# Sparse attention with global tokens and a feed-forward: global scores of a quad in one operation with band scores

## The chip, the cores and the metric

The kernel runs on one core of a Trainium2 chip. The metric is the device time of one execution in microseconds, from three runs: the median is compared. The trace is one further execution, recorded by the hardware profiler.

## The reference

Eight batches of eight heads; each head has 512 local and 32 global tokens of 64 values. A local query sees the local keys at most 32 positions away and all 32 global keys; a global query sees every key. What comes out, 4352 rows of 512 values, goes through a feed-forward layer with 2048 hidden values.

```python
def _attn_ref(q_l, k_l, v_l, q_g, k_g, v_g):
    ...
    k_all = np.concatenate([k_g, k_l], axis=2)
    v_all = np.concatenate([v_g, v_l], axis=2)
    s_g = scale * np.matmul(q_g, k_all.transpose(0, 1, 3, 2))
    out_g = np.matmul(sm(s_g), v_all)
    s_ll = scale * np.matmul(q_l, k_l.transpose(0, 1, 3, 2))
    mask = np.abs(pos[:, None] - pos[None, :]) <= window
    s_ll = np.where(mask, s_ll, -1000000000.0)
    s_lg = scale * np.matmul(q_l, k_g.transpose(0, 1, 3, 2))
    a_l = sm(np.concatenate([s_lg, s_ll], axis=-1))
    out_l = np.matmul(a_l, v_all)
    return np.concatenate([out_g, out_l], axis=2)

def _moe_ref(x, w_in, w_out):
    h = x @ w_in
    g = h - np.tanh(h)
    return g @ w_out
```

`sm` is the softmax over the last axis.

## The kernel before

**Tiling.** Two heads make a pair, so there are 32 pairs, `pairs[0]` to `pairs[31]`, four to a batch; two pairs make a quad. The feed-forward works in chunks: one for each batch's 512 local rows and one, at the end, for the 256 global rows of all batches. A chunk of 512 rows has 16 steps; a step has twelve hidden matmuls (line 1219, or 1245 in the earliest steps) and twelve output matmuls (line 1282), each of 512 columns: the float32 operands are split in a high and a low part, and three of the four products are made. Between the two stand ACT's tanh (1227), DVE's subtraction (1230), a rounding copy (363, ACT mostly) and the rest, taken on POOL (1236). The attention of batch b+1 runs among the feed-forward of batch b.

**Attention from the ninth pair on** (`j >= OWN`, `OWN` is 8). For each pair, `add_keys` and `add_queries` transpose the raw keys and queries on DVE (697, 709). `add_band_scores` (713) makes the local scores: a block of 32 queries against 96 local keys and the 32 global keys, 32 matmuls of 64 rows, 32 stationary columns and 128 moving columns, in two operations, the first of two 128-row tiles and the second of the other two; the scores of the two heads stand in two banks. `add_band` (1126) follows with peak (DVE, 1132), exponential (ACT, 1137), inverse (DVE) and scaling (POOL, 1146), and transposes the result (DVE, 1152), which DMAs move to where the products read it. For each quad, `Quad.add_halves` (955) makes the scores of the global queries of its four heads, 16 matmuls in the same 64-row, 32-column shape, eight with 256 moving columns and eight with 32 (line 972), in two further banks, and then peak (DVE, 982 and 985), exponential (ACT, 993), inverse and scaling (POOL, 1003). `add_global_turn` (779) transposes them on DVE (793, 795), and `add_products` (800) multiplies all probabilities of a pair by its values (830). The trace counts two records for each of these matmuls: 64 for a pair's band, 32 for a quad's global scores.

**Earlier pairs.** Pairs 4 to 7 use the same band scores, but other global scores (`add_scores`, 1016, with the matmuls at 1030) and other products (814). Pairs 0 to 3 have a path of their own (`first_attention`: 547, 656, 1176).

**Banks.** There are eight banks of matmul results. Operations ask for banks from a named set (line 356): attention of later batches from `att`, banks 0 to 2; hidden layer from `h`, banks 0 to 3; output layer from `acc`, banks 4 to 7.

**The order.** No operation is issued where the program names it. Each is handed to `add` with its engine and estimated time, what it reads and writes, the banks that it takes and frees, and a due time. `Order.run` (115) then simulates the engines and repeatedly takes the operation with the earliest start (plus a small share of its due time), and the instructions are issued in that order on each engine's queue. A bank is handed out only when whoever held it has been placed with all that read it. Going from one tile shape of TensorE to another is charged by `switch` (101): `MW` for the way back to the full array, `MV` for others. When TensorE would idle early on, `filler` (1507) puts matmuls without use in the gap. The due times and weights are the constants of `CFG` (343): names that begin with `o_` and end in 0, 1 or 2 are the offsets of attention in the first batch, the second and all later ones (`o_l`: band scores, `o_g`: global scores), and the rest set weights loading, the steps of the feed-forward, and which engine is preferred for a copy.

`attention(j)` (1389) names the operations of a pair in sequence; where two of them touch the same buffer, this sequence decides which is first. For odd `j` it names, after the keys, the quad's global scores, the turning and products of the pair before, and then the queries and the band scores of pair `j`.

Of the kernel before, what the change touches and what calls it, by code (L numbers as in the profile page):

```python
# [217 lines left out]
def kernel(ctx, tc, q_l, k_l, v_l, q_g, k_g, v_g, w_in, w_out, out):  # L218
# [3 lines left out]
    NT = S // P  # L222
    T = S + G
# [12 lines left out]
    OWN = 8  # L236
# [94 lines left out]
    def bank(shape, j, dt=F32):  # L331
# [6 lines left out]
        elif len(shape) == 4:  # L338
# [1 line left out]
        return t  # L340


    CFG = dict(a_g=-20, a_kg=8.6471, a_ph=-0.3776, a_qs=3.1395, a_w=0.1186, a_wn=0.3468, a_xg=106.4499, d_g=3.1804, d_kg=30.2528, d_ph=13.5028,
               d_qh=26.732, d_qs=-2.8448, d_tg=-7.2746, d_tp=19.0976, d_w=27.3757, d_wn=73.5687, d_xg=31.5443, d_y=19.0351, gfirst=0, ho=4086.9099,
               hs=1945.7008, lag=2058.0703, last=-656.3726, newb=2, p0=1174.4585, pen=-2.1431, penp=-16.7696, s_g=37.3966, s_w=10.8784,
               step=4056.6186, step1=117.929, lag0=-6898.385, hs0=174.1645, tol=0.0001449392, wd0=3738.22, wsp=-399.3218, xw=0.07263301,
               o_ld0=6998.8548, o_tn0=-70.3794, o_tg0=4900.3517, o_s0=-8488.5413, o_sp0=-1339.9745, o_t0=-7480.9842, o_vl0=-4568.2292,
               o_pv0=-6980.563, wsp1=-266.4844, ho0=4731.2006, mw=0.2696114, o_h0=9000, hp=-9000, bp0=8995.7209, bp1=-7509.0482, bp2=-3805.4551,
               bp3=-9000, p_w=150, p_kg=-0.4636, mv=0.0001195388, kd=3.441514e-05, a_sq=8.5297, o_gb=8757.2134, o_kl2=-2217.8445, o_ql2=7034.0784,
               o_kt2=-7538.1981, o_qt2=-1378.049, o_l2=-5351.7965, o_lp2=-2940.782, o_g2=-2834.6403, o_tg2=-1206.1443, o_sq2=-696.1794,  # L350
               o_vl2=5851.8969, o_pv2=8097.3484, o_kl1=2328.5123, o_ql1=5480.9611, o_kt1=-1133.8937, o_qt1=-1536.1301, o_l1=-8243.7002,
               o_lp1=4742.1478, o_g1=7959.6348, o_tg1=7293.7765, o_sq1=6170.1166, o_vl1=-3483.3411, o_pv1=310.4111, o_g0=-5056.3219, p_bd=33.4845)

    PHASE = [{k[:-1]: v for k, v in CFG.items() if k.startswith("o_") and k.endswith(x)} for x in "012"]

# [1 line left out]
    add = order.add  # L357
# [142 lines left out]
    class Pair:  # L500
# [209 lines left out]

            add(("D", 0.69), turn, self.due(self.C["o_qt"]), r=["kq"], w=["hk0"])

        def add_band_scores(self, *ranges):
            kw, u = keys[self.u], self.u
            s = [(f"s{a.two}", a.i) for a in self.heads]
            box = {}

            def mm(tiles):
                def fn(e, tags):
                    if "s" not in box:  # L720
                        box["s"] = [bank([P, NT, SQ], tags[x]) for x in s]
                        for a in self.heads:
                            a.scores = box["s"][a.two]
                    for t in tiles:
                        for c in range(4):
                            n = NT * t + c - 1
                            at = G * (2 + 3 * (n // 2) + n % 2 if n >= 0 else 0)
                            for a in self.heads:
                                r = slice(a.e, a.e + D)
                                nc.tensor.matmul(box["s"][a.two][G * c:G * c + G, t], query()[r, t * P + G * c:t * P + G * c + G],  # L730
                                                 kw()[r, at:at + SQ], start=True, stop=True)
                return fn

            for j, tiles in enumerate(ranges):
                add(("T", 0.222 * len(tiles)), mm(tiles), self.due(self.C["o_l"] + self.C["o_lp"] * j), r=[f"kw{u}", f"kg{u}", "hk0"], w=s,
                    res=["p00", "p10"],
                    alloc=[(x, "att") for x in s] if j == 0 else (), rows=0.8, ldw=0.027, tail=0.107, mode=3)
            for a in self.heads:
                a.add_band(self)
# [208 lines left out]
    class Quad:  # L948
# [3 lines left out]
            self.m, self.pairs = m, pairs[2 * m:2 * m + 2]  # L952
            self.sn = 2 * (m % 2)

        def add_halves(self):
            a, b, c, d = [stats[self.sn + i][:, j:j + 2] for i in range(2) for j in (12, 14)]
            sg, sh, st = ("sg", self.m, "q"), ("sh", self.m, "q"), ("st", self.sn)
            all_ = ["pg0", "pg1", "pl0", "pl1"]
            box = {}
            C = self.pairs[0].C  # L960

            def mm(e, tags):
                box["s"] = y = [bank([P, 9 * G], tags[n]) for n in (sg, sh)]
                for lo, n in ((0, 8 * G), (8 * G, G)):
                    for x in self.pairs:
                        for half in range(2):
                            p0 = 64 * x.u + G * half
                            for r in range(2):
                                rows = slice(64 * r, 64 * r + 64)
                                k = keys[x.u]()[rows]  # L970
                                k = k[:, G:2 * G] if lo else view(k[:, :1], [(3 * G, 4), (1, 2 * G)], 2 * G + 12 * G * half)
                                nc.tensor.matmul(y[r][p0:p0 + G, lo:lo + n], gqs()[rows, 0, x.jj, r], k, start=True, stop=True)  # L972

            def swap(dst, src):
                for q in range(4):
                    p = slice(32 * q, 32 * q + 32), slice(32 * (q ^ 1), 32 * (q ^ 1) + 32)
                    nc.vector.tensor_copy(dst[p[0]], src[p[1]])  # L977

            def peak(e, _):
                zero = masks[1][:, WIN:WIN + 1]  # L980
                for r in range(2):
                    nc.vector.tensor_tensor_reduce(out=pgh[:, r, G:9 * G], in0=box["s"][r][:, :8 * G], in1=zero.broadcast_to([P, 8 * G]), scale=-0.125,
                                                   scalar=1e30, op0=ALU.add, op1=ALU.min, accum_out=a[:, r:r + 1])
                for r in range(2):
                    nc.vector.tensor_tensor_reduce(out=pgh[:, r, 9 * G:], in0=box["s"][r][:, 8 * G:], in1=only_first, scale=-0.125,
                                                   scalar=a[:, r:r + 1], op0=ALU.add, op1=ALU.min, accum_out=b[:, r:r + 1])
                swap(c, b)
                nc.vector.tensor_tensor(a, b, c, op=ALU.min)

            def exp(e, _):  # L990
                for r in range(2):
                    x = pgh[:, r, G:]
                    nc.scalar.activation(x, x, AF.Exp, bias=a[:, r:r + 1], scale=-1.0, accum_out=c[:, r:r + 1])

            def inverse(e, _):
                swap(b, c)
                nc.vector.scalar_tensor_tensor(d, c, 1e-9, b, op0=ALU.add, op1=ALU.add)
                nc.vector.reciprocal(b, d)

            def norm(e, _):  # L1000
                for r in range(2):
                    x = pgh[:, r, G:]
                    nc.gpsimd.tensor_scalar(x, x, b[:, r:r + 1], 1.0, op0=ALU.mult, op1=ALU.mult)

            def due(off):
                return self.pairs[1].due(C["o_g"] + off)

            reads = [f"{n}{u}" for n in ("kw", "kg") for u in range(2)] + ["gq"]
            pool = self.pairs[0].tag
            add(("T", 0.53), mm, due(0), r=reads, w=[sg], res=all_, alloc=[(sg, pool), (sh, pool)], ldw=0.027, tail=0.027, rows=0.8, mode=3)  # L1010
            add(("D", 2.05), peak, due(1), r=[sg, ("mask", 1), "of"], w=all_ + [st], free=[(sg, 1), (sh, 1)])
            add(("A", 1.15), exp, due(1.5), r=[st], w=all_)
            add(("D", 1.1), inverse, due(2), r=["pg0"], w=[st])
            add(("P", 1.25), norm, due(2.5), r=[st], w=all_)

        def add_scores(self):
            if self.m >= OWN // 2:
                return self.add_halves()
            s = stats[self.sn]
            sg, sh, st = ("sg", self.m, "q"), ("sh", self.m, "q"), ("st", self.sn)  # L1020
            all_ = ["pg0", "pg1", "pl0", "pl1"]
# [367 lines left out]
    def attention(j):  # L1389
        order.land = LAND  # L1390
        x = pairs[j]
        if j == OWN:
            add_gaps()
        x.add_keys()
        if j % 2:
            quad = Quad(j // 2)
            quad.add_scores()
            pairs[j - 1].add_global_turn()
            pairs[j - 1].add_products(0, 1)
        x.add_queries()  # L1400
        x.add_band_scores(*(range(2), range(2, NT)))
        if j + 1 < NH // 2:
            if (j + 1) % (H // 2) == 0:
                add_globals((j + 1) // (H // 2))
            pairs[j + 1].add_raw()
        if j % 2 == 0:
            x.add_values()
        x.add_squares()
        if j % 2:
            x.add_values()  # L1410
            x.add_global_turn()
            x.add_products(0, 1)
# [133 lines left out]
```

## Time and profile before

| what | value |
|---|---|
| median of three runs | 904.38 us (903.88 to 907.87) |
| profiled execution, its own time | 905.91 us |
| its span, first to last instruction | 904.1 us |
| TensorE (PE) busy | 892.7 us, 99% |
| VectorE (DVE) busy | 481.7 us, 53% |
| ScalarE (ACT) busy | 372.5 us, 41% |
| GpSimd (POOL) busy | 338.9 us, 37% |
| granted TensorE clock, mean | 0.993 |

Busy is the union of an engine's instructions. Matmuls overlap, so a busy TensorE is not one at its peak: how far it comes is read from the distance between the starts of successive groups. Times of a timeline count from the span's first instruction.

### The profile page before, as it was taken

The numbers are of one execution on the slowest core, as the hardware profiler recorded it, in microseconds if no ns is written. First come the engines' busy times: TensorE is split into PE (matmuls) and PEld (weight loads), VectorE is DVE, ScalarE is ACT, GpSimd is POOL, SyncE is SP. The second block draws the span as 40 slices with busy tenths as digits, with TensorE's granted clock in tenths as the row PEclk, the third lists the DMA queues.
The fourth block names the chain that finished last, engine by engine and source line by source line (L and its number), as shares of the span: only waits on it lengthen the run. The fifth ranks groups of instructions, "written<-read, shape, count | busy, mean of one in ns | idle before, by whom it ended". The sixth has DMA issues, their size and how long they took to land.

```text
span 904.1 us, 23449 instructions
## 1 busy us (share of the span) xinstructions
PE 892.7 (99%) x9100; PEld 719.8 (80%) x9100; DVE 481.7 (53%) x1820; ACT 372.5 (41%) x1035; POOL 338.9 (37%) x504
## 2 busy tenths in 40 slices
PE   8999999999999999999999999999999999999998
PEld 6678787787878888787878888788878888888896
DVE  6889977835638383745638373746637362111110
ACT  6877764434344333533343333533344242322221
POOL 5567665333333233333333233423223231222121
PEclk9899999999999999999999999999999999999999
DMA  9877774934555434555555434545454302100000
GB/s 207 192 185 204 205 182 98 226 92 112 107 135 139 101 85 112 142 117 116 103 153 116 109 84 111 144 114 119 95 147 112 95 35 61 47 1 1 36 13 23
DMA packets 286959, 101.14 MB, mean 112 GB/s; under 512 B 254848, under 2 KB 277376, under 8 KB 286848
## 3 DMA queue, kind: packets, MB, share of 16 engines
q1 hardware_dynamic: 284800, 98.53, 45.5%
q8 instruction: 71, 1.16, 0.5%
q10 hardware_dynamic: 2048, 1.11, 0.4%
q14 instruction: 40, 0.33, 0.1%
HBM read 76.01 MB, written 21.50 MB: 108 GB/s over the span
## 4 chain that ended last, share of the span: by engine, by line
PE 92%; DVE 4%; ACT 2%; issue 1%; DMA 1%; POOL 0%; ACTq 0%; DVEq 0%; POOLq 0%
PE bank L1282 40%; PE bank L1219 39%; PE bank L830 4%; PE bank L730 3%; PE bank L814 2%; PE bank L1245 1%; PE bank L656 1%; PE bank L1176 1%; PE bank L972 1%; DVE turned L793 1%; DVE stats L977 1%; DMA raw<-in_q_l_dram 1%; DVE t L1230 0%; ACT prob L1137 0%; PE bank L547 0%
## 5 line engine op out<-in xcount | busy, mean ns | idle before, releaser
L1236 POOL TENSOR_TENSOR gates<-t,gates 128x512 fp32r<-128x512 f32 x136 | 175.1, 1288 | 394.0 <-PE bank L1282 245.7
L1282 PE MATMUL bank<-w_out_hi,gates 128*128 128x512 f32 x1088 | 297.2, 393 | 0.9 <-ACT gates L363 0.9
L1282 PEld LDWEIGHTS bank<-w_out_hi,gates 128*128 128x128 f32 x1088 | 202.3, 188 | 46.9 <-issue 2.9
L1230 DVE TENSOR_TENSOR t<-bank,t 128x512 f32<-128x512 f32 x136 | 92.8, 684 | 238.8 <-ACT t L1227 238.3
L1227 ACT ACTIVATE t<-bank 128x512 f32<-128x512 f32 x136 | 80.7, 594 | 232.2 <-PE bank L1219 231.2
L363 ACT CAST gates<-t 128x512 fp32r<-128x512 f32 x136 | 84.3, 622 | 166.9 <-PE bank L1282 92.8
L1282 PE MATMUL bank<-w_out_lo,gates 128*128 128x512 f32 x544 | 150.8, 391 | 0.0
L1219 PE MATMUL bank<-x_hi,w_in_hi 128*128 128x512 f32 x432 | 123.4, 401 | 0.0
L1282 PEld LDWEIGHTS bank<-w_out_lo,gates 128*128 128x128 f32 x544 | 102.0, 188 | 21.8 <-issue 0.2
L1219 PE MATMUL bank<-x_lo,w_in_hi 128*128 128x512 f32 x432 | 118.6, 390 | 0.0
L1219 PE MATMUL bank<-x_hi,w_in_lo 128*128 128x512 f32 x432 | 118.5, 390 | 0.0
L1146 POOL TENSOR_SCALAR prob<-prob,stats 128x128 f32<-128x128 f32 x224 | 79.0, 372 | 82.5 <-DVE stats L1142 43.7
L1137 ACT ACTIVATE prob<-prob,stats 128x128 f32<-128x128 f32 x224 | 86.9, 390 | 22.8 <-DVE stats L1132 22.8
L1219 PEld LDWEIGHTS bank<-x_lo,w_in_hi 128*128 128x128 f32 x432 | 81.0, 188 | 17.7 <-issue 0.2
L1219 PEld LDWEIGHTS bank<-x_hi,w_in_lo 128*128 128x128 f32 x432 | 80.9, 188 | 17.8 <-issue 0.2
L1219 PEld LDWEIGHTS bank<-x_hi,w_in_hi 128*128 128x128 f32 x432 | 77.8, 188 | 19.3 <-issue 2.8
L793 DVE STREAM_TRANSPOSE turned<-pg 32x96 f32<-32x96 f32 x288 | 77.7, 270 | 8.5 <-PE bank L830 1.7
L1132 DVE CUSTOM_DVE_ANT_0 prob<-bank,band 128x128 f32<-128x128 f32 x224 | 49.7, 286 | 28.1 <-PE bank L730 28.1
L1152 DVE STREAM_TRANSPOSE sq<-prob 128x512 f32<-128x512 f32 x50 | 35.3, 708 | 51.3 <-POOL prob L1146 48.7
L1137 ACT ACTIVATION_READ_ACCUMULATOR prob<-prob,stats 128x1 f32 x224 | 42.1, 188 | 0.0
L830 PEld LDWEIGHTS bank<-turned 128*32 128x32 f32 x3072 | 33.4, 111 | 8.9 <-issue 5.7
L830 PE MATMUL bank<-turned 128*32 128x32 f32 (+1 forms) x3072 | 37.2, 206 | 0.1
(157 smaller groups left out, 900.1 us busy)
## 6 DMA issues: line engine op xcount, KB each, us to landing
moved<-sq SPq DMA_DIRECT2D x24, 512.0 KB, 2.8
turned<-in_v_l_dram SPq DMA_DIRECT2D x23, 512.0 KB, 5.4
turned<-in_v_l_dram SPq DMA_DIRECT2D x32, 256.0 KB, 3.5
out_dram<-wraw SPq DMA_DIRECT2D x32, 256.0 KB, 2.1
rawkq<-in_k_l_dram SPq DMA_DIRECT2D x112, 64.0 KB, 2.6
rawkq<-in_q_l_dram SPq DMA_DIRECT2D x112, 64.0 KB, 2.4
turned<-in_v_g_dram SPq DMA_DIRECT2D x48, 128.0 KB, 4.6
turned<-moved SPq DMA_DIRECT2D x48, 128.0 KB, 2.9
```

Of the source, the lines that this page charges most:

```text
L363: (nc.scalar.copy if e == "A" else eng[e].tensor_copy)(dst, src)
L793: nc.vector.transpose(win_g[G * g:G * g + G, a.two, 3 * x:3 * x + 3], view(pgh[r, a.two, G * (j + x):G * (j + x) + 1], [(3 * G, 3), (1, G)]))
L830: m = nc.tensor.matmul(y, win_v[:, NW * a.two + w, G * d:G * d + G], x, start=n == 0, stop=n == 7, skip_group_check=True)
L1132: nc.vector.tensor_tensor_reduce(out=x[:, t], in0=self.scores[:, t], in1=bands[0 if t == 0 else 2 if t == NT - 1 else 1], scale=-0.125, sc ...
L1137: nc.scalar.activation(x[:, t], x[:, t], AF.Exp, bias=self.st[:, t:t + 1], scale=-1.0, accum_out=self.st[:, 4 + t:5 + t])
L1146: nc.gpsimd.tensor_scalar(x[:, t], x[:, t], self.st[:, 8 + t:9 + t], 1.0, op0=ALU.mult, op1=ALU.mult)
L1152: nc.vector.transpose(z[:, :, self.two].rearrange("p n t c -> p t n c"), x[:, :, k * n * G:(k + 1) * n * G].rearrange("p t (n c) -> p t n ...
L1219: nc.tensor.matmul(self.h[s][:, j * n:(j + 1) * n], w[:, cc, f * P:(f + 1) * P], self.x()[xi](cc)[:, :n], start=part == 0 and cc == 0 and ...
L1227: nc.scalar.activation(tt_[q], self.h[s], AF.Tanh)
L1230: nc.vector.tensor_sub(tt_[q], self.h.pop(s), tt_[q])
L1236: eng[e].tensor_sub(gg[q][1], tt_[q].rearrange("p (k c) -> p k c", k=4), f32(gg[q][0]))
L1282: nc.tensor.matmul(self.acc[tt], g[:, j * nt + tt], low_out(f) if wi else w_out_hi[:, f], start=s == 0 and k == 1, stop=last and k == 3 * ...
```

## The change

Global scores of the quads from the ninth pair on (twelve quads, at odd `j` from 9 to 31) are no longer an operation of their own. `add_band_scores` of the quad's second pair hands its matmuls, all four tiles at once, to `add_halves`, which issues them and then the global scores in one operation. This operation asks for four banks of the set `h`, where there were two of `att` for each. Its due time is that of the band scores. In `attention`, the quad's turning and products of its first pair are named after the band scores of the second. Band scores of the first pair of a quad stay as two operations, and so do all of the pairs before the ninth. All constants of `CFG` that set the order get other values, also those of the first batch and of the loading of weights; of those lines one is shown.

```diff
-               o_pv0=-6980.563, wsp1=-266.4844, ho0=4731.2006, mw=0.2696114, o_h0=9000, hp=-9000, bp0=8995.7209, bp1=-7509.0482, bp2=-3805.4551,
+               o_pv0=-698.2739, wsp1=-397.8031, ho0=6683.6544, mw=0.6734363, o_h0=1583.6807, hp=-2528.881, bp0=8787.3597, bp1=-7359.1769,
...
-        def add_band_scores(self, *ranges):
+        def add_band_scores(self, *ranges, quad=None):
...
-            for j, tiles in enumerate(ranges):
+            if quad:
+                quad.add_halves(mm(range(NT)), self.due(self.C["o_l"]), s, [f"kw{u}", f"kg{u}", "hk0"])
+            for j, tiles in enumerate(() if quad else ranges):
                 add(("T", 0.222 * len(tiles)), mm(tiles), self.due(self.C["o_l"] + self.C["o_lp"] * j), r=[f"kw{u}", f"kg{u}", "hk0"], w=s,
...
-        def add_halves(self):
+        def add_halves(self, scores, at, s, more):
...
-            pool = self.pairs[0].tag
-            add(("T", 0.53), mm, due(0), r=reads, w=[sg], res=all_, alloc=[(sg, pool), (sh, pool)], ldw=0.027, tail=0.027, rows=0.8, mode=3)
+            def both(e, tags):
+                scores(e, tags)
+                mm(e, tags)
+
+            add(("T", 0.888 + 0.53), both, at, r=reads + more, w=[sg] + s, res=all_ + ["p00", "p10"], alloc=[(x, "h") for x in s + [sg, sh]],
+                ldw=0.027, tail=0.027, rows=0.8, mode=3)
...
         def add_scores(self):
-            if self.m >= OWN // 2:
-                return self.add_halves()
...
         if j % 2:
             quad = Quad(j // 2)
-            quad.add_scores()
+            if j < OWN:
+                quad.add_scores()
+                pairs[j - 1].add_global_turn()
+                pairs[j - 1].add_products(0, 1)
+        x.add_queries()
+        x.add_band_scores(*(range(2), range(2, NT)), quad=quad if j % 2 and j >= OWN else None)
+        if j % 2 and j >= OWN:
             pairs[j - 1].add_global_turn()
             pairs[j - 1].add_products(0, 1)
-        x.add_queries()
-        x.add_band_scores(*(range(2), range(2, NT)))
```

## Rows read from the trace of the kernel before

**Rows 1.** The page, chain that ended last, by engine and by line.

```profile
PE 92%; DVE 4%; ACT 2%; issue 1%; DMA 1%; POOL 0%; ACTq 0%; DVEq 0%; POOLq 0%
PE bank L1282 40%; PE bank L1219 39%; PE bank L830 4%; PE bank L730 3%; PE bank L814 2%; PE bank L1245 1%; PE bank L656 1%; PE bank L1176 1%; PE bank L972 1%; DVE turned L793 1%; DVE stats L977 1%; DMA raw<-in_q_l_dram 1%; DVE t L1230 0%; A
```

**Rows 2.** Windows: stretch, length, busy us by engine, granted clock, DMA share, GB/s.

```profile
0.00:60.60 60.60, 54.43 (x444) 40.84 (x444) 46.71 (x195) 45.33 (x129) 33.76 (x70) 0.92 0.87 198
...
140.00:760.30 620.30, 619.30 (x7269) 496.87 (x7267) 345.83 (x1374) 236.08 (x703) 214.78 (x339) 1.00 0.49 115
...
37.00:46.00 9.00, 8.70 (x51) 6.38 (x53) 7.58 (x36) 7.21 (x22) 5.75 (x10) 0.62 0.88 206
```

**Rows 3.** Timeline of PE around a quad's global scores: start, length, what.

```profile
419.21 1.07 PE L1282 MATMUL bank<-w_out_lo,gates 128*128 128x512 f32 x4
420.12 1.07 PE L1282 MATMUL bank<-w_out_hi,gates 128*128 128x512 f32 x4
421.12 0.42 PE L972 MATMUL bank<-kw,qgt 64*32 64x256 f32 x4
...
421.36 0.40 PE L972 MATMUL bank<-kw,qgt 64*32 64x256 f32 x4
...
421.57 0.21 PE L972 MATMUL bank<-kw,qgt 64*32 64x32 f32 x4
...
421.77 0.96 PE L1219 MATMUL bank<-x_hi,w_in_hi 128*128 128x512 f32 x3
...
422.80 0.85 PE L1219 MATMUL bank<-x_lo,w_in_hi 128*128 128x512 f32 x3
```

**Rows 4.** Timeline of PE around the band scores of that quad's second pair.

```profile
413.33 1.07 PE L1282 MATMUL bank<-w_out_hi,gates 128*128 128x512 f32 x4
414.33 1.16 PE L730 MATMUL bank<-hl,hi 64*32 64x128 f32 x64
415.42 0.96 PE L1219 MATMUL bank<-x_hi,w_in_hi 128*128 128x512 f32 x3
...
416.45 0.85 PE L1219 MATMUL bank<-x_lo,w_in_hi 128*128 128x512 f32 x3
```

**Rows 5.** Groups of PE, line 730, one buffer: busy us, mean ns.

```profile
L730 PE MATMUL bank<-hl,hi 64*32 64x128 f32 x896 | 16.5, 274 | 0.0
```

**Rows 6.** Windows, line 972 alone, first and last quad: PE, PEld, clock, DMA.

```profile
153.00:156.00 3.00, 0.72 (x32) 0.49 (x32) 1.00 0.19 49
...
730.00:732.00 2.00, 0.72 (x32) 0.49 (x32) 1.00 0.00 0
```

**Rows 7.** Timeline of PE, band scores of the last pair.

```profile
720.90 1.16 PE L730 MATMUL bank<-hl,hi 64*32 64x128 f32 x64
```

**Rows 8.** Timeline of ACT, DVE and POOL, 411 to 424 us.

```profile
411.78 0.60 ACT L1227 ACTIVATE t<-bank 128x512 f32<-128x512 f32 x1 [2.65 <-PE bank L1219]
412.41 0.69 DVE L1230 TENSOR_TENSOR t<-bank,t 128x512 f32<-128x512 f32 x1 [2.72 <-ACT t L1227]
413.53 0.62 ACT L363 CAST gates<-t 128x512 fp32r<-128x512 f32 x1 [1.15 <-PE bank L1282]
414.55 1.28 POOL L1236 TENSOR_TENSOR gates<-t,gates 128x512 fp32r<-128x512 f32 x1 [5.87 <-PE bank L1282]
415.52 0.29 DVE L1132 CUSTOM_DVE_ANT_0 prob<-bank,band 128x128 f32<-128x128 f32 x1 [2.42 <-PE bank L730]
...
417.22 0.08 DVE L1132 DVE_READ_ACCUMULATOR2_ANT stats<- 128x1 f32 x1
...
422.00 0.42 DVE L982 CUSTOM_DVE_ANT_0 pg<-bank,mask 128x256 f32<-128x256 f32 x1 [0.62 <-PE bank L972]
...
423.04 0.08 DVE L985 DVE_READ_ACCUMULATOR2_ANT stats<- 128x1 f32 x1
```

**Rows 9.** Timeline of PE, first stage.

```profile
36.87 1.00 PE L1176 MATMUL bank<-idr,prob 128*128 128x128 f32 x4 [1.18 <-POOL prob L1117]
```

**Rows 10.** Timeline, 164 to 170 us, TensorE's wait.

```profile
168.55 1.20 PE L1282 MATMUL bank<-w_out_hi,gates 128*128 128x512 f32 x4 [0.63 <-ACT gates L363]
```

More of the change, by code (lines that the diff above doesn't have):

```diff
@@ L340, in bank @@
         return t
[L343 to L347, printed above, removed]
-               o_pv0=-6980.563, wsp1=-266.4844, ho0=4731.2006, mw=0.2696114, o_h0=9000, hp=-9000, bp0=8995.7209, bp1=-7509.0482, bp2=-3805.4551,
[L349 to L352, printed above, removed]
@@ new lines @@
+    CFG = dict(a_g=-4.2124, a_kg=0.9209, a_ph=0.1045, a_qs=-10.4157, a_w=0.2849, a_wn=-10.1521, a_xg=150, d_g=43.5019, d_kg=4.7833, d_ph=6.0967,
+               d_qh=26.732, d_qs=0.9416, d_tg=-12.1384, d_tp=48.2891, d_w=33.4823, d_wn=-1.8283, d_xg=53.7677, d_y=0.5952, gfirst=0, ho=4236.1957,
+               hs=1756.827, lag=1298.9946, last=-1097.129, newb=2, p0=1600.6077, pen=40.9401, penp=13.2212, s_g=90.9463, s_w=148.4937,
+               step=3626.2582, step1=232.186, lag0=-7573.8374, hs0=320.0268, tol=8.870367e-05, wd0=4621.609, wsp=-231.304, xw=1.801357e-06,
+               o_ld0=3976.404, o_tn0=-2260.2415, o_tg0=6987.204, o_s0=-8426.0597, o_sp0=-1339.9745, o_t0=-7982.7618, o_vl0=1978.8146,
+               o_pv0=-698.2739, wsp1=-397.8031, ho0=6683.6544, mw=0.6734363, o_h0=1583.6807, hp=-2528.881, bp0=8787.3597, bp1=-7359.1769,
+               bp2=-2687.6789, bp3=-8791.7452, p_w=16.9945, p_kg=0.7975, mv=0.001661925, kd=3.748658e-05, a_sq=8.5297, o_gb=3097.1763,
+               o_kl2=2197.6687, o_ql2=1414.084, o_kt2=5159.0148, o_qt2=9000, o_l2=-7506.4833, o_lp2=1250.4435, o_g2=-4619.084, o_tg2=5545.905,
+               o_sq2=-2849.1106, o_vl2=-6908.976, o_pv2=6351.1419, o_kl1=8189.4185, o_ql1=1909.5038, o_kt1=-3778.3009, o_qt1=-2125.2221,
+               o_l1=-8287.3901, o_lp1=3977.886, o_g1=1189.308, o_tg1=8769.6804, o_sq1=-1050.6185, o_vl1=-2042.2736, o_pv1=1427.2712,
+               o_g0=2344.6175, p_bd=37.4079)
```

## The prediction

> **What bounds the kernel now.** I read the chain of work first, then the windows by stage, then TensorE's own timeline around the work that the change touches. The chain is TensorE for 92% of the span, and most of that is the two lines of the feed-forward part [rows 1]. The windows say where this holds [rows 2]. From 140 to 760.3 us TensorE is busy for 619.30 of 620.30 us at a granted clock of 1.00, so in this stage the time is the amount of TensorE's work and the way in which it is packed, and no other engine is near (DVE 346, ACT 236, POOL 215 us). The first 60.6 us are another regime: 6 us without a matmul, clock 0.92, DMA share 0.87. All twelve quads that the change touches lie in the first of these two stages; the constants that set the order reach into both.
>
> **What an attention operation costs beside its own work.** Feed-forward matmuls come in groups of four, one group each 0.91 us (419.21 to 420.12) [rows 3]. So each operation between them can be priced by how far it pushes the next group. Band scores of one pair: the last group before them starts at 413.33, so the next was due at 414.24. The band's matmuls start at 414.33, the feed-forward returns at 415.42, and its second group starts at 416.45, that is 1.03 us later and not 0.91 [rows 4]. The price is 416.45 - 0.91 - 414.24 = 1.30 us, of which the band's own stretch is 1.09 and the two rims 0.09 + 0.12 = 0.21. A quad's global scores, by the same sum: due 421.03, start 421.12, return 421.77, second group 422.80 [rows 3], so 422.80 - 0.91 - 421.03 = 0.86 us, with a stretch of 0.65 and rims of 0.21 again. Together a quad pays 2.16 us.
>
> **Part 1: the two in one operation.** Both are 64-row by 32-column matmuls, so nothing forces the array to empty between them. Gone is one pair of rims, 0.21 us. Gone too is the tail of the band: its 64 records last 1.16 us and one of them about 0.27 (TensorE's own groups give 274 ns [rows 5]), so the last one starts 0.89 us after the first, while the feed-forward begins only 1.09 us after it. Records follow each other every 0.89 / 63 = 0.014 us, eight of them at a time in eight tiles, so the first global record could start at about 0.90: 0.19 us saved. The first set of 256-column records holds its tiles for 0.24 us, the second for 0.21 (by the starts at 421.12 and 421.36, and 421.57) [rows 3]; if the extra 0.03 belongs to the entry it goes as well. The saving is then 0.21 + 0.19 = 0.40, with the 0.03 it is 0.43, and at the very best the whole difference between the global stretch and its streaming, which I put at 0.46 by adding as much again. Least it is 0.21, if the band's tail stays. I take 0.43, because all three pieces are read off one quad and the twelve global stretches are alike: 0.72 us busy in each, from the first to the last [rows 6]. In none of them do the global scores touch the band of the same quad today: 5.7 us of feed-forward lie between in the quad shown (415.42 to 421.12) [rows 3, 4], 8.4 in the last one, whose band starts at 720.90 and takes 1.1 [rows 7], and at least 3 in the ten others. So the saving is there twelve times: 12 x 0.43 = 5.2 us, bounds 12 x 0.21 = 2.5 and 12 x 0.46 = 5.5. Nothing covers it up: TensorE has no waits in this stage into which a gain could fall, and ahead of the last feed-forward part it stays the bound.
>
> **Part 2: four banks at once.** Today the global scores take two of banks 0 to 2 and the band two of them, some us apart; the merged operation wants banks 0 to 3 all free. The hidden layer lives in these banks too. Two waits are new. Before the operation, the subtraction of the last hidden group must have been made: ACT's tanh at 411.78 takes 0.60, DVE's subtraction at 412.41 takes 0.69 [rows 8], so the bank is free at 413.10, while the output matmuls behind that hidden group run until 414.24. With those between, the wait costs nothing, with 1.1 us to spare; without that cover it is up to 1.4 us. After it, the next hidden group needs a bank back, and what stands behind the merged operation on TensorE is all the feed-forward. DVE reads a band bank in four instructions, eight for the pair from 415.52 to 417.30 [rows 8], so the first bank returns about 1.0 us after the feed-forward's start, and a global pair takes from 422.00 to 423.12. If an output group of 2.7 us stands next, all of this is hidden; if a hidden group stands next, it waits. Today it is a hidden group that follows the global scores (421.77 [rows 3] stands for eleven of twelve). The output group's own operands come from ACT and POOL (0.62 and 1.28 us [rows 8]) after the subtraction, 1.9 us in all, most of which the merged operation's own stretch of about 1.5 covers. So a clean order exists; I take zero for this part, bounds 0 and 1.0 to 1.35 us for each quad.
>
> **Part 3: the rest of the edit.** Turning the probabilities of the first pair's global rows and its products are added after the band instead of ahead of it; the trace already runs band, global scores, products in that order, so it moves nothing by itself. The DMAs issued for values, squares and raw keys keep their place in the text and their queue (SP); only their due times change. The weight on leaving a tiled mode (mw) goes from 0.27 to 0.67, which could join further operations, and could also hold TensorE for one that isn't ready. The first 60.6 us are ordered by new constants too. What that can do is bounded by what is loose there: between 37 and 46 us the granted clock is 0.62, that is 9 x 0.38 = 3.4 us lost [rows 2]; ahead of it TensorE idled for 1.18 us and ran short transposes [rows 9]. An order that keeps TensorE fuller there gains up to 3.4, one that opens another such stretch loses about as much. I see no sign for either and take zero.
>
> **The sum.** The profiled execution took 905.91 us, a span of 904.1 and 1.8 around it; 905.91 - 5.2 = 900.7. The median of the runs is 904.38, that is 1.5 lower, so the forecast is 904.4 - 5.2 = 899.2.
>
> **Rivals.** (a) The order of the beginning shifts by one stretch at half clock, for the better 904.4 - 5.2 - 3.4 = 895.8, for the worse 902.6. For it: the constants of that stage change widely. Against: one attention chain sets that stage, and it isn't edited.
> (b) The merge doesn't do what it says: the array empties between band and global scores although the tile shape is one. Only the rims are saved, 2.5 us, 901.9. For it: each set of records brings new weights and other rows. Against: the band's own sets follow each other at 0.014 us per record, set after set of eight.
> (c) Gate stalls eat it. At 168.55 TensorE stood 0.63 us for ACT's cast while DVE and ACT were in the band's work [rows 10]; the merged operation hands DVE 1.8 + 1.1 us of peaks in one go, so subtraction, tanh and cast queue behind them. Seven or eight such stalls cost 4.7 us: 903.9. Against: only one in 620 us today.
> (d) The other side, slower: banks. If at each quad a hidden group stands behind the merged operation, it waits 1.0 to 1.35 us for DVE to hand back a bank, 12 to 16 us, less 5.2: 911 to 915, say 912. It turns the sign as soon as the wait passes 0.43 us. For it: today's order has a hidden group there in eleven cases. Against: output groups alternate with hidden ones, use other banks (4 to 7), and their operands are ready.
> The Trainium skill, TensorEngine Tiling (Array Packing), section Performance Considerations, speaks for (d): tiling makes TensorE faster but not the reading of its banks, so that emptying them can become the bound. The trace has the size of it: 1.09 us of band matmuls against 1.78 us of DVE peaks [rows 4, 8]. By that rule alone the next hidden group would wait in each quad and the time would be that of (d); by the row it holds only where no output group of 2.7 us stands between.
>
> **How the numbers follow.** Forecast (899.2, give or take 1.5 for a small shift of the order) 0.48; (a) better 0.14, worse 0.10; (b) 0.10; (c) 0.10; (d) 0.08. A difference of 0.5% is 4.5 us, about what a measurement of this kernel can tell from no change: 899.9. The forecast stands only 0.7 us beyond it, so three quarters of its chance count as faster: 0.37, with (a) better 0.51, say 0.52. Its rest, (a) worse, (b) and (c) make 0.40 of no change, (d) 0.08 slower. The range reaches from (a) better to just past (c), 895.0 to 904.5, and leaves out (d) and the ends of (a).
>
> **What would show it.** In the trace after: twelve blocks of global scores with no feed-forward matmul ahead of them, starting within 0.03 us of the band's last record; a merged stretch near 1.55 us in place of 1.09 + 0.65; a stage without waits of TensorE of above 0.2 us behind those blocks; 5 us less from the first such quad to the end of attention. If TensorE shows idle time ended by DVE's peaks, (d) is right; ended by ACT's cast, (c). If the gain or loss already stands at 60 us, it is (a), and the prediction is wrong where I took zero for the new constants.

## The result, and the profile after

The changed kernel takes 897.8 us against 904.9 of the kernel before, each the median of four runs; the ratio is 0.9913, 95% interval 0.9900 to 0.9926. Measured again in two later sessions beside the kernel before, it gave 898.9 against 904.8 (0.9934, 0.9919 to 0.9948) and 899.8 against 905.6 (0.9935, 0.9918 to 0.9952). The gain is 6 to 7 us, 0.65 to 0.9%.

The page of the changed kernel: span, busy time of each engine, and the chain that ended last.

```profile
span 896.0 us, 23423 instructions
...
PE 884.5 (99%) x9098; PEld 720.6 (80%) x9098; DVE 483.6 (54%) x1819; ACT 374.6 (42%) x1038; POOL 341.2 (38%) x502
...
PE 95%; ACT 2%; DMA 1%; DVE 1%; issue 0%; POOL 0%; ACTq 0%; POOLq 0%; DVEq 0%
```

Its windows by stage, which answer to [rows 2] (stretch, length, busy us of PE, PEld, DVE, ACT and POOL, granted clock, DMA share, GB/s).

```profile
0.00:59.10 59.10, 52.17 (x442) 39.04 (x442) 45.79 (x193) 47.03 (x136) 32.78 (x66) 0.94 0.87 201
...
140.00:752.20 612.20, 611.89 (x7240) 497.99 (x7241) 348.57 (x1377) 235.47 (x695) 214.25 (x336) 1.00 0.50 116
```

TensorE stays the bound: attention ends 8 us earlier, and from 140 us to there TensorE is busy in all but 0.3 us. Where twelve times a band and a quad's global scores stood apart, they now stand as this. The timeline of PE around one merged operation, to be laid beside [rows 3, 4]; in this kernel line 731 is the band, 975 the global scores, 1224 the hidden and 1287 the output matmuls.

```profile
252.20 1.08 PE L1287 MATMUL bank<-w_out_hi,gates 128*128 128x512 f32 x4
253.21 1.16 PE L731 MATMUL bank<-hl,hi 64*32 64x128 f32 x64
254.11 0.41 PE L975 MATMUL bank<-kw,qgt 64*32 64x256 f32 x4
...
254.33 0.41 PE L975 MATMUL bank<-kw,qgt 64*32 64x256 f32 x4
...
254.54 0.24 PE L975 MATMUL bank<-kw,qgt 64*32 64x32 f32 x7
...
254.79 1.19 PE L1287 MATMUL bank<-w_out_hi,gates 128*128 128x512 f32 x4
255.83 0.85 PE L1287 MATMUL bank<-w_out_lo,gates 128*128 128x512 f32 x3
```

The global records begin 0.90 us after the band's first, where in [rows 4] the feed-forward came back only after 1.09. The whole stretch is 254.79 - 253.21 = 1.58 us. By the way of reckoning of the prediction the next group was due at 253.11, and the second one behind starts at 255.83, so the price is 255.83 - 0.91 - 253.11 = 1.81 us in place of 2.16. Read a few groups further behind, both prices settle a little higher or stay, and the difference is 0.37 to 0.39; I use 0.38. All twelve are alike, stretch 1.58, the first at 165.53 and the last at 709.55, and all twelve have output matmuls behind them.

How long the stage takes is best read between two operations that stand at the same place in both orders: the first whole band operation behind the first 60 us, and the products of the last pair. In the first trace of the kernel before the timeline of PE gives

```profile
71.90 1.16 PE L730 MATMUL bank<-hl,hi 64*32 64x128 f32 x64
...
760.29 1.54 PE L830 MATMUL bank<-turned 128*32 128x64 f32 x128
```

760.29 - 71.90 = 688.4 us, and in a second trace of it

```profile
72.06 1.16 PE L730 MATMUL bank<-hl,hi 64*32 64x128 f32 x64
...
759.69 1.54 PE L830 MATMUL bank<-turned 128*32 128x64 f32 x128
```

687.6 us. In the changed kernel the same two rows are

```profile
70.26 1.16 PE L731 MATMUL bank<-hl,hi 64*32 64x128 f32 x64
...
752.17 1.54 PE L833 MATMUL bank<-turned 128*32 128x64 f32 x128
```

681.9 us, and in its second trace

```profile
70.70 1.16 PE L731 MATMUL bank<-hl,hi 64*32 64x128 f32 x64
...
752.84 1.54 PE L833 MATMUL bank<-turned 128*32 128x64 f32 x128
```

682.1; a third trace of it has 682.4. So 6.0 us of the gain lie in this stage by the four traces shown, with a spread of about 0.5 us either way. Behind the stage all five traces take 143.8 us, so the rest of the gain, 0 to 1 us by the medians, lies ahead of it. Of the 6.0, twelve merges at 0.38 make 4.6. The other 1.4 are odd waits which the new order doesn't have:

- In both traces of before, four products start late, 0.06 us behind the end of DVE's last turning (in the first trace at 281.06, 382.31, 483.69 and 584.94). They begin 0.42 to 0.45 us after the last feed-forward record began, where the other twenty, and all in the changed kernel, take 0.32. Together this is 0.4 and 0.5 us.
- In both, TensorE waits 0.6 us for ACT's cast ([rows 10]), against 0.3 in the changed kernel, and one band (161.64 in the first) takes 0.33 and 0.39 us longer than all others.
- In the first trace alone, products at 157.21 take 0.44 longer.

That is 1.5 us in the first trace and 1.2 in the second, and the changed kernel's second trace has one wait of 0.3 more than its first. With the 4.6 it leaves 0.4 of the 6.5 us between the first traces unexplained, and hardly any of the 5.5 between the second ones.

### The profile page after: what moved, and what is told of

The parts are those of the page before. It is cut to its first block, busy times and chain, and to the rows that moved or that the text cites. A ratio compares the mean times of both kernels' runs of the same rounds, so it can differ in the third digit from the quotient of the medians.

```text
span 896.0 us, 23423 instructions
## 1 busy us (share of the span) xinstructions
PE 884.5 (99%) x9098; PEld 720.6 (80%) x9098; DVE 483.6 (54%) x1819; ACT 374.6 (42%) x1038; POOL 341.2 (38%) x502
## 4 chain that ended last, share of the span: by engine, by line
PE 95%; ACT 2%; DMA 1%; DVE 1%; issue 0%; POOL 0%; ACTq 0%; POOLq 0%; DVEq 0%
PE bank L1287 42%; PE bank L1224 40%; PE bank L833 4%; PE bank L731 3%; PE bank L817 1%; PE bank L1250 1%; PE bank L657 1%; PE bank L975 1%; PE bank L1181 1%; DMA wraw<-in_moe_w_in_dram 1%; DMA raw<-in_q_l_dram 0%; PE bank L548 0%; ACT turned L364 0%; PE bank L588 0%; ACT prob L1116 0%
## 5 line engine op out<-in xcount | busy, mean ns | idle before, releaser
L1224 PE MATMUL bank<-x_hi,w_in_hi 128*128 128x512 f32 x432 | 119.8, 393 | 0.0
L1224 PEld LDWEIGHTS bank<-x_hi,w_in_hi 128*128 128x128 f32 x432 | 80.1, 188 | 18.2 <-issue 0.6
```

Source lines behind the costliest of these rows:

```text
L1224: nc.tensor.matmul(self.h[s][:, j * n:(j + 1) * n], w[:, cc, f * P:(f + 1) * P], self.x()[xi](cc)[:, :n], start=part == 0 and cc == 0 and ...
```

## The experiments

The theory to test: what is saved at each quad is one way out of the tiled shape and back, with the band's tail, about 0.39 us, and the order of the feed-forward hides what four banks at once cost. Its rivals: the new constants alone made the gain, and the banks bind. The column stage is the stretch between the two operations named above, in the profiled execution. Medians stand beside those of the kernel before on the same chip.

| kernel | median us | before, same chip | ratio, 95% interval | stage us |
|---|---|---|---|---|
| constants alone | 907.1 | 905.2 | 1.0029 (1.0013 to 1.0045) | 689.6 |
| merge alone | 903.3 | 905.2 | 0.9977 (0.9968 to 0.9987) | 687.1 |
| seam broken | 905.7 | 905.2 | 1.0010 (0.9999 to 1.0021) | 688.9 |
| hidden group next | 903.0 | 905.2 | 0.9970 (0.9957 to 0.9983) | 686.5 |
| changed, again | 898.9 | 904.8 | 0.9934 (0.9919 to 0.9948) | 682.4 |
| scores swapped | 900.9 | 904.8 | 0.9955 (0.9938 to 0.9972) | 683.9 |
| further join | 906.2 | 904.8 | 1.0018 (1.0005 to 1.0031) | 687.3 |
| short tail | 899.5 | 905.6 | 0.9938 (0.9923 to 0.9954) | 683.0 |
| changed, once more | 899.8 | 905.6 | 0.9935 (0.9918 to 0.9952) | 682.1 |
| further join, shifted | 908.2 | 905.4 | 1.0023 (1.0008 to 1.0037) | 687.9 |

### The two halves of the change: constants alone, merge alone

The kernel before with the constants of the changed one:

```diff
-    CFG = dict(a_g=-20, a_kg=8.6471, ...)
+    CFG = dict(a_g=-4.2124, a_kg=0.9209, ...)
```

> The kernel before with the new constants of the order, without the merge. Theory (the merge pays 0.39 us at each of twelve quads, 4.7 us, the rest of the 7 us is the beginning and a few odd waits): the beginning gains its 1.5 us here too, the twelve separate global operations cost 0.88 us each as before, and the time is 901 to 905 us. Rival (the new constants alone bring the gain): 897 to 899 us.

It took 907.1 us, 2 us more than before: both the range of the theory and the rival's were missed, the rival's by far. The global operations stand alone again at 0.87 us each, and the order brings waits of its own. Who TensorE waited for between 61 and 762 us (us in total, times, longest):

```profile
PE bank L1283 <- ACT gates L364: 1.3, 1, 1.3
PE bank L731 <- DVE xg L857: 0.8, 2, 0.6
PE bank L831 <- DVE turned L796: 0.2, 1, 0.2
```

The stage is 1.6 us longer than in the kernel before. The trace is of the fastest of twelve executions, 905.4 us; where the others lose up to 6 us more isn't shown. So the constants by themselves are worth nothing, even a little less than the old ones.

The changed code with the constants of before:

```diff
-    CFG = dict(a_g=-4.2124, a_kg=0.9209, ...)
+    CFG = dict(a_g=-20, a_kg=8.6471, ...)
```

> The merge with the constants of the kernel before. Theory in its plain form (the merge pays by itself): 905 - 4.7 = 900 us, and the merged operations cost 1.8 us each. Rival (four banks at once want an order made for them): the merged operations cost the same 1.8 us, but TensorE stands behind or ahead of some of them until DVE hands back a bank, 1 us and more each, and the time is 902 to 906 us.

It took 903.3 us: 1.9 less than before, which lies in the rival's range, but for the most part not for its reason. The merged operations have the same stretch of 1.58 us, but for one, 2.18, behind which a hidden group waits. The same view of waits:

```profile
PE bank L832 <- DVE turned L797: 3.1, 4, 0.9
PE bank L1223 <- DVE stats L1136: 0.5, 1, 0.5
PE bank L1286 <- ACT gates L363: 0.3, 1, 0.3
```

The large term isn't the one that the rival named. Four times TensorE stands ahead of a pair's products (832) for DVE's turning of the global rows (797). The timeline of PE at the first of the four:

```profile
279.22 0.98 PE L832 MATMUL bank<-turned 128*32 128x64 f32 x76 [0.90 <-DVE turned L797]
```

and at the same quad in the kernel before, where these products already start 0.1 us late:

```profile
281.06 1.56 PE L830 MATMUL bank<-turned 128*32 128x64 f32 x128
```

With the global scores now tied to the band, the last turning at these four quads ends 15.9 to 16.1 us behind the start of the global scores, against 11.8 in the kernel before, and the products of the old order stand too early for it. In the changed kernel it ends 11.8 to 12.7 us behind, and the products come 4.7 us or more after it in eleven of the twelve quads (0.9 in the first): that is what the new order does. In the merge alone 3.1 + 0.5 us, with smaller waits ahead of 100 us, take back most of the 4.6. Together the two halves gain 6 to 7 us, alone +2 and -2: the merge makes the gain possible, the order lets it through.

### What was saved: the seam broken

```diff
             def both(e, tags):
                 scores(e, tags)
+                nc.tensor.matmul(bank([P, 4, P], tags[sg]), idr, idr.unsqueeze(1).broadcast_to([P, 4, P]), start=True, stop=True)
                 mm(e, tags)
```

> The changed kernel with one full-array matmul of 512 columns between band scores and global scores inside each merged operation; the order is untouched. Theory (what was saved is leaving and entering the tiled shape and the band's tail, 0.39 us): each merged operation costs 0.39 + 0.23 (the matmul itself) = 0.62 us more, twelve of them 7.4 us, so about 905 us. Rival (the array empties at the seam anyway, the gain came from the order): only the matmul's own 0.23 and at most the rims, 2.7 to 5 us, 900.5 to 903 us.

905.7 us, and a stage of 688.9 us against 682.0 (the mean of the two traces shown above), 6.9 more. Timeline of PE at one of the twelve; line 1014 is the matmul put between.

```profile
254.57 1.16 PE L731 MATMUL bank<-hl,hi 64*32 64x128 f32 x64
255.65 0.50 PE L1014 MATMUL bank<-idr 128*128 128x512 f32 x1
256.08 0.42 PE L975 MATMUL bank<-kw,qgt 64*32 64x256 f32 x4
...
256.74 1.20 PE L1288 MATMUL bank<-w_out_hi,gates 128*128 128x512 f32 x4
```

The stretch grows from 1.58 to 256.74 - 254.57 = 2.17 us, by 0.59, of which 0.23 is a 512-column matmul in its row (a quarter of a group's 0.91). The band is back at 1.08 us, as when it stood alone, and the global scores at 0.66. Twelve times 0.59 are 7.1 us: the theory's 7.4 and the measured 6.9 agree, the rival's 2.7 to 5 are out. One full-array matmul at the seam undoes the merge: beside its own work it costs 0.36 us, of the 0.38 that were saved.

### The banks: a hidden group behind the merged operation

The plan was made as in the changed kernel, and then, in the list of operations, the output groups behind six of the twelve merged operations were put behind the next hidden group.

```diff
         out.sort(key=lambda v: v[:2])
+        for m in [v[2] for v in out if v[2] is not None and v[2].fn.__name__ == "both"]:
+            ...
+            out[:] = [v for k, v in enumerate(out[:last + 1]) if k not in outs] + held + out[last + 1:]
```

> The changed kernel, but behind six of the twelve merged operations the next hidden group is issued ahead of the output groups that stood there. Theory (the output groups hide the time in which DVE hands back the banks): TensorE stands 1.0 to 1.35 us at each of the six, 6 to 8 us, so 904 to 906 us, and the other six show no wait. Rival (banks come back in time in any order): 898 us, no idle time behind the merged operations.

903.0 us, and a stage of 686.5, 4.5 more than the changed kernel. The waits of TensorE between 61 and 762 us, and the timeline at one of the six (754 band, 998 global scores, 1160 and 1008 their peaks, 1247 hidden):

```profile
PE bank L1247 <- DVE stats L1160: 3.2, 6, 0.5
PE bank L1310 <- ACT gates L387: 1.2, 2, 0.8
PE bank L1247 <- DVE sq L461: 0.8, 1, 0.8
```

```profile
256.58 1.16 PE L754 MATMUL bank<-hl,hi 64*32 64x128 f32 x64
...
257.77 0.29 DVE L1160 CUSTOM_DVE_ANT_0 prob<-bank,band 128x128 f32<-128x128 f32 x1 [3.14 <-PE bank L754]
...
258.62 0.42 DVE L1008 CUSTOM_DVE_ANT_0 pg<-bank,mask 128x256 f32<-128x256 f32 x1
...
258.76 1.20 PE L1247 MATMUL bank<-x_hi,w_in_hi 128*128 128x512 f32 x4 [0.53 <-DVE stats L1160]
```

The six stand still and the other six don't, which is the theory; the price is half of what was expected. The stretch is 2.18 us in place of 1.58, so 0.60 each and 3.6 for six. DVE begins on the band's bank at 257.77, when the band's matmuls are done and the global ones still run, not when the operation ends at 258.16. The remaining 0.9 us are the last row, a wait near 101 us for DVE's work on the weights, that this execution had and the changed kernel's first didn't; the longest wait for a cast lies ahead of the stage.

### The same shapes the other way round

```diff
             def both(e, tags):
-                scores(e, tags)
                 mm(e, tags)
+                scores(e, tags)
```

> The changed kernel with the global scores ahead of the band scores inside each merged operation; the order is untouched. Theory (what counts is the one shape, not which comes first): a merged operation costs 1.8 us within 0.05 and the time is that of the changed kernel within 1 us. Rival (the short 32-column records at the end hide the way back to the full array): 0.1 us more each, 1.2 us in all.

900.9 us, 2.0 more than the changed kernel on the same chip. The timeline of PE:

```profile
253.77 0.42 PE L975 MATMUL bank<-kw,qgt 64*32 64x256 f32 x4
...
254.29 0.27 PE L731 MATMUL bank<-hl,hi 64*32 64x128 f32 x1
...
254.41 1.16 PE L731 MATMUL bank<-hl,hi 64*32 64x128 f32 x63
255.51 1.20 PE L1287 MATMUL bank<-w_out_hi,gates 128*128 128x512 f32 x4
```

The stretch is 1.74 us, 0.16 longer, twelve times 1.9 us, and so much longer is the stage. The global scores take 0.64 and the band 1.10, each as long as alone. One record of the band does start at 254.29, while the last of the global ones run, but its other 63 come only from 254.41 on. Only the rims are saved, as the prediction's rival (b) had it, but for the swapped sequence. My theory, that only the common shape counts, is wrong.

I took the short records at the end of the global scores for the reason: they would let the array change back sooner. So the last tile of each band that stands alone was split into 96 and 32 columns:

```diff
-                    for t in tiles:
+                    parts = [(t, 0, SQ) for t in tiles]
+                    if not quad and tiles[-1] == NT - 1:
+                        parts[-1:] = [(NT - 1, 0, 3 * G), (NT - 1, 3 * G, SQ)]
+                    for t, lo, hi in parts:
```

> The changed kernel; in the band operations that stand alone (15 behind the first 60 us) the last tile's scores are made in two sets of records, 96 columns and then 32, so that they end as the merged operations do. Theory (short records at the end let the full array come back earlier, 0.15 us by the swapped order): each costs 1.32 - 0.15 + 0.03 (eight records more) = 1.2 us, 1.5 to 2 us in all, 896.5 us beside 898. Rival (what the swap lost lies between the two shapes of scores, not at the end): 1.32 us and more, 898 to 899 us.

899.5 us, beside 899.8 of the changed kernel on the same chip; the stage is 0.9 longer. The timeline of PE around one of the fifteen:

```profile
277.00 1.22 PE L734 MATMUL bank<-kw,hi 64*32 64x128 f32 x80
278.15 1.21 PE L1290 MATMUL bank<-w_out_hi,gates 128*128 128x512 f32 x4
```

The stretch grew from 1.09 to 1.15 us: sixteen records more, no earlier return. The short records are not the reason. What makes the seam from band to global scores 0.16 us cheaper than the one back, and what holds the band's other records for 0.13 us, isn't settled.

### A further join, and where it went

If rims are the price, products (128 rows by 32 columns) and the next pair's band (64 by 32) in one operation should save a pair of them too.

```diff
+            if past:
+                past.add_global_turn()
+                past.add_products(0, 1, join=(mm(range(NT)), self.due(self.C["o_l"]), s, [f"kw{u}", f"kg{u}", "hk0"]))
...
+                def both(e, tags):
+                    mm_windows(e, tags)
+                    scores(e, tags)
```

> The changed kernel with one more join: from the tenth pair on, the products of a quad's second pair (128 rows by 32 columns) and the band scores of the next pair (64 by 32) stand in one operation over banks 0 to 3, eleven times. The tile shapes differ, so the array must still change over. Theory (a join saves one pair of rims, 0.21 us, even where the shape changes, and the drain stays): 11 x 0.2 = 2.3 us less than the changed kernel, 895.5 us. Rival (the change of shape costs as much as the way over the full array, or the four banks bring waits): 898 us or more.

906.2 us, slower than both. Six of the eleven joins went nearly as expected: their stretch is 2.56 us (one 2.68), the products' 1.47 and the band's 1.09 each as alone, and their price 2.78 against 1.71 + 1.30 = 3.01 for the two, 0.23 saved. The other five stood still in the middle and took 3.49 to 4.61 us, together 8.1 more; less the 11 x 0.23 = 2.5 saved that is 5.6, and the stage is 5.3 longer. Timeline of PE, one of these (836 products, 731 band):

```profile
342.12 1.54 PE L836 MATMUL bank<-turned 128*32 128x64 f32 x128
343.59 0.63 PE L731 MATMUL bank<-kw,hi 64*32 64x128 f32 x22
...
345.91 0.89 PE L731 MATMUL bank<-kw,hi 64*32 64x128 f32 x42 [1.69 <-issue]
```

"issue" says that the profile shows nothing that TensorE waited for. Over the stage it is 6.3 us in five stops. The DMA view of 343.2 to 344.5 us has the only thing that moves then: one packet of 16 KB on the queue of kind instruction.

```profile
q8 instruction: 1, 0.02, 5.1%
```

The whole program has 71 of these for the 18,196 matmuls and weight loads that its trace counts, 256 to a packet; each of the five stops ends 1.3 to 1.5 us after the end of such a packet. A join takes 192 matmuls and as many weight loads, 384 instructions in 2.6 us. To test it, 128 instructions without use were put behind the program's first matmuls, half a packet:

```diff
                 nc.tensor.matmul(bank([P, 4, P], tags["warm"]), x, x.unsqueeze(1).broadcast_to([P, 4, P]), start=True, stop=True)
+            for j in range(32):
+                nc.tensor.matmul(bank([P, 512], tags["warm"])[:32, :32], f32(x)[:64, :32], f32(x)[:64, :32], start=True, stop=True)
```

> The kernel with the further joins once more, with 32 tiny matmuls (64 records, each a weight load and a matmul, so 128 instructions) put behind the very first matmuls of the program; their results are not used. In the trace of the joins TensorE stood 0.6 to 1.7 us in five of eleven with nothing to wait for, in the joins that began 74 to 164 instructions into a block of 256, counted from the start of TensorE's records, and in none of the others (2 to 54 and 184 to 200). Theory (its instructions come too late: a join takes 384 of them in 2.6 us): half a block later the stops move to the second, sixth, seventh and eleventh join (near 241, 444, 490 and 698 us), and are gone from the five that had them; 1 to 3 us less than without the shift. Rival (data or banks make those five wait): the stops stay where they are.

The stops moved as said: the five joins that had them have none (stretch 2.54 to 2.56), and the second, sixth, seventh and eleventh are 1.9, 0.4, 1.8 and 0.7 us longer; the fifth, which began 182 instructions into a block, is 2.3 longer and wasn't named. Timeline of PE at the second, and then at the fourth, the one shown above:

```profile
244.61 1.54 PE L836 MATMUL bank<-turned 128*32 128x64 f32 x128
246.08 0.66 PE L731 MATMUL bank<-kw,hi 64*32 64x128 f32 x31
248.42 0.73 PE L731 MATMUL bank<-kw,hi 64*32 64x128 f32 x33 [1.68 <-issue]
...
346.40 1.54 PE L836 MATMUL bank<-turned 128*32 128x64 f32 x128
347.87 1.16 PE L731 MATMUL bank<-kw,hi 64*32 64x128 f32 x64
```

The time of that kernel, 908.2 us, didn't fall by the 1 to 3 us expected: the five stops make 7.1 us in place of 8.1, the stage is as long as without the shift (687.9 and 687.3), and the first whole band comes at 76.5 us, later than in every other trace (70.2 to 73.7). The supply of instructions is the cause of the stops: where they fall follows the blocks. Neither version with this join beats the changed kernel.

### The same kernels again

> The changed kernel once more, beside the kernel before on the same chip as the runs below. Theory: 897 to 899 us, 7 us below the kernel before; of this 6 to 6.6 us lie behind the first 60 us. What the trace of the first 60 us says is open: the same order ended them at 59.0 to 60.9 us in three other kernels, so a difference of 1.5 us there is within what one order does from run to run.

898.9 us, 5.9 below the kernel before. In its trace, of an execution of 901.7 us, the stage is 682.4, but the first whole band comes only at 73.7 us.

> The kernel before, looked at once more. Theory (the 1.5 us that the first 60 us took longer in its trace are no property of its order): the feed-forward's 25th matmul starts at another time than 60.6, 59.2 to 60.5 us, while the stretch from there to the last products stays 701 us within 0.5. Rival (its order costs 1.5 us there): 60.6 again.

Its first whole band came at 72.06 us, as late as in the first trace (71.90), and its 25th feed-forward matmul at 59.3 in place of 60.6, with the granted clock at half from 59.6 to 63 us. From that matmul to the last products it took 0.7 us longer than in the first trace, a little more than the 0.5 named.

> The changed kernel once more on this chip, for its trace. Theory: from the feed-forward's hundredth matmul to the last products 675.7 us within 0.5, as in its first trace, against 681.8 in the kernel before; the time ahead of that differs by up to 2 us between executions of one order.

The stage is 682.1 us, and the stretch named here agrees with that of the first trace within 0.2. Ahead of it, one order gives different times: the first whole band comes at 70.2 to 73.7 us in eight traces that share the changed kernel's order up to there (its own three, seam, hidden group, swapped, further join, constants alone), and at 70.4 to 72.1 in three that share the old one.

## Why the prediction was right, step by step

The forecast was 899.2 us, the range 895.0 to 904.5, faster as the likeliest. Measured: 897.8, and later 898.9 and 899.8.

- **Part 1, the merge.** Right in kind and a little too large: 0.38 us a quad for 0.43, 4.6 us for 5.2. The global records do start 0.90 us after the band's first, as reckoned. The stretch is 1.58 us for the 1.55 that was named. The 0.03 that I put down to the entry of the global scores is saved: their first set of 256 columns now takes 0.22 (254.11 to 254.33) for 0.24. But from the first 32-column record to the feed-forward's return it is 0.25 (254.54 to 254.79) for 0.20 in [rows 3]: the eight records of a set start mostly 17 ns apart there, and 7 ns apart where the global scores stand alone. The sum had no term for this. That the saving comes from the seam is shown by the broken seam.
- **The lower bound of part 1**, rims alone, is what the swapped sequence measures: 2.0 us lost of 4.6.
- **Part 2, the banks.** Zero was right: all twelve have output matmuls behind them, none waits. That a clean order existed was argued from the lengths of the operations, and as to the banks even the old constants found it for eleven of the twelve (merge alone). The bound of 1.0 to 1.35 us was too high, it is 0.60: I let DVE begin at the end of the operation, and it begins at the end of the band. Rival (d) with this price would be, by estimate, twelve times 0.60 less 4.6, about 907 us and not 912. Of rival (c), ACT's cast, one wait of 0.3 us is left in the stage.
- **Part 3, the new constants.** Taking zero for them was wrong as a step, though its result stood. They cost 2 us without the merge, and with it they gain 5 (687.1 to 682.0 in the stage). The wait that they remove, products that stand ahead of DVE's turning, I had looked at and dismissed, because the order band, global scores, products stays, and Part 1 held that TensorE has no waits into which a gain could fall. But four products already stood right behind that turning, 0.1 us late, and what moves is when the turning is done (16 us behind the global scores in the old order, and not 11.8) and how far behind it the products stand. On (a), the first 60 us, nothing is shown: one order spreads over 3.5 us there, and the medians leave 0 to 1 us.
- **The sum.** 4.6 us of merges and 1.4 of odd waits make the 6.0 of the stage. The second term wasn't in the forecast, and that it made up for the first one's shortfall of 0.6 is luck.
- **The rule of the Trainium skill** that I weighed (TensorEngine Tiling (Array Packing), Performance Considerations: emptying the banks can become the bound) doesn't decide here: where a hidden group stands next the wait is 0.60 us, where an output group stands next it is nothing.

## What to carry to other kernels

Price a small operation between large ones by how far it pushes the next of these, and split that price into its own work, the two rims and the tail; a merge saves the rims, and the tail only in a sequence that has to be tried. When a merge ties results together that were apart, look for who gets them later (here the products, by DVE's turning), since that is where the gain was lost in the old order. And before joining many tiny matmuls, count their instructions: here 192 in 1.58 us came through, and so did the 256 of the products alone in 1.47; the 384 of a join in 2.6 us didn't in five of eleven. So it is the length of the burst, and not its pace alone, that counts.

## What the runs showed of the hardware that was not expected

- TensorE ran dry of instructions in a stream of 192 small records: stops that made a join 0.4 to 2.3 us longer, most of it called "issue" by the profile, whose place moved with the place of the program's 256-instruction packets. The Trainium skill (Runtime: NRT & Kernel Launch, Instruction fetch mechanics) has the blocks of 256 as measured here and calls the cost of crossing one mostly hidden; in these joins it isn't.
- From band to global scores, both 64 by 32, the records run on without a gap (0.90 us); from global scores to band all but one of them don't (0.64, as alone). The common tile shape alone doesn't give the overlap.
- Two tile shapes in one operation (128 by 32, then 64 by 32) save about 0.23 us, a pair of rims, and no tail.
